# Deeper loading of raw 64-bit weights in the first block, borrowed homes for three of seven, and a last block ordered by segments

## The chip, the cores and the metric

The kernel runs on one core of a Trainium2 chip. The metric is the device time of one execution in microseconds, and what stands for a kernel is the median over its runs. Before the change that is 948.53 us, the median of 3 runs that lie between 947.35 and 951.66 us.

## The reference, cut to what matters

```
q, k, v: (4, 8, 576, 64) float32
q_d, k_d, v_d = mean over groups of 4 positions              # 144 positions
out_up    = repeat(softmax(q_d k_d^T / 8) v_d, 4)            # coarse attention
out_local = softmax over |i - j| < 4 of (q k^T / 8), times v # banded attention
x = (out_up + out_local) as (2304 tokens, 512)
g = x @ w_gate;  x2 = (silu(g) * (x @ w_val)) @ w_out        # 512 -> 1536 -> 512
h = x2 @ w_in
out = (h * clip(h + 3, 0, 6) / 6) @ w2_out                   # 512 -> 2048 -> 512
```

The five weight matrices arrive as 64-bit floats; everything else is 32-bit.

## The kernel before, in words

**Blocks.** The 2304 tokens are 36 units of 64 tokens. `BLOCKS = [8, 6, 8, 8, 6]` cuts them into five blocks of 512 or 384 tokens. The tokens of batch 0 (9 units) are computed by `first_batch`, whose instructions stand in the order of the table `FRONT`; the attention of the other batches runs beside the matrix products of the block before the one that needs it. It is cut into chunks (`CUTS`): for each, `load_chunk` issues loads of q, k and v on SyncE's queue, `chunk_scores` multiplies q by seven shifted k on VectorE (tile `pr`, line 852) and reduces (`sc`, line 855).

**Products.** Each block runs 68 weight units of 12 matmuls (9 for P in a 384-token block): G and V (gate and value, `pG`, `pV`), O (first output, `aO`), H (second input, `pH`), P (second output, `aP`). They are numbered through, so 4 and 5 are G, 6 and 7 V, 8 and 9 O, 10 and 11 G, 12 and 13 V, 14 and 15 O. Every weight is split into a high and a low part of type fp32r, every input too, and three of the four partial products are made.

**The way of a weight in block 0.** `load_raw` loads the 64-bit words (512 KB a unit, tile `w64`, four buffers; line 220) on SyncE's queue, `decode_a` takes the sign and exponent on ScalarE (`top`, line 237), `decode_b` makes 32-bit words on VectorE (`w`, line 246; it also frees the raw buffer), `split_hi` (ScalarE, `wr`, line 264) and `split_lo` (VectorE, `wr`, line 269) make the two parts for a pair of units, and ScalarE's queue writes the 32-bit pair to DRAM (`kept`). Blocks 1 to 4 load the kept pair (512 KB) and split it again. `prefetch(i)` does these steps for units ahead of i: loading by `LR = 8`, decoding by 5 and 4, splitting by 3.

**What else matters here.** `first_batch` keeps the softmax weights in `held`, a tile in the buffer of `x2`, and a temporary `tmp` in one of the two buffers of `xr`, the columns of the block's input. `x2` holds the output of the first network at the end of a block's first half, and `os`, the output, takes its buffer after that. Instructions stay in program order on their engine; a DMA that waits for its buffer holds up all behind it on SyncE's queue. `put_out` copies 128 output rows from PSUM (line 1073 on VectorE for odd quarters of the last block, 1075 on ScalarE) and stores them (line 1084).

Of the kernel before, what the change touches and what calls it, by code (L numbers as in the profile page):

```python
# [11 lines left out]
F32 = mybir.dt.float32  # L12
F32R = mybir.dt.float32r
# [14 lines left out]
BLOCKS = [8, 6, 8, 8, 6]  # L28

CUTS = [[3, 2], [2, 2, 2, 2], [3, 2, 3], [3, 3], []]  # L30
LR, LD, LA, LB, LS = 8, 6, 5, 4, 3
WARM = 14
CLOAD = (2, 6)

# [28 lines left out]
def tile_kernel(  # L63
# [124 lines left out]
    w32 = {}  # L188
    split = {}

    def load_raw(i):
        if units[i][2] == 0:
            load_unit(i)
# [5 lines left out]
    def load_unit(i):  # L199
        kind, f, bi = units[i]  # L200
        if bi or not wide:
            if i % 2 == 0:
                w32[i // 2] = sp.tile([P, 2, DM], F32, tag="wst", name=f"w32_{i}", bufs=3)
        if bi:
            if i % 2 == 0:
                nc.sync.dma_start(w32[i // 2], kept[i % NU // 2])
            return
        src = wsrc[kind]
        if wide:
            src = src.bitcast(I16)  # L210
        m = 4 if wide else 1
        if kind in "GVH":
            h = i % 2
            src = src[h * DM // 2:(h + 1) * DM // 2, (f - h) * P * m:(f - h + 2) * P * m]
            src = src.rearrange("(c p) f -> p c f", p=P)
        else:
            src = src[f * P:(f + 1) * P, :].rearrange("p (c e) -> p c e", c=2)
        if wide:
            raw[i] = sp.tile([P, 4 * DM + 32], I16, tag="w64", name=f"w64_{i}", bufs=4)
            behind(nc.sync.dma_start(raw[i][:, 1:1 + 4 * DM].rearrange("p (c e) -> p c e", c=2), src))  # L220
        else:
            nc.sync.dma_start(w32[i // 2][:, i % 2].rearrange("p (c e) -> p c e", c=2), src)
# [49 lines left out]
        split[i], split[i + 1] = r[:, 0], r[:, 1]  # L272

    def prefetch(i):
        steps = ((LR, load_raw), (LD, load_kept), (LA, decode_a), (LB, decode_b), (LS, split_unit))
        for ahead, fn in steps:
            if i + ahead < len(units):
                fn(i + ahead)
# [18 lines left out]
    xr = {}  # L297
    x_done = [0]

    def columns(bi, col, xv):  # L300

        if bi not in xr:
            xr[bi] = sp.tile([P, NC, 2, UMAX * UT], F32R, tag="xr", name=f"xr{bi}")
        return xr[bi][:, :, :, col:col + xv.shape[2]]

    def put_cols(bi, col, xv):

        dst = columns(bi, col, xv)
        nc.scalar.activation(dst[:, :, 0], xv, AF.Copy)  # L309
        nc.vector.tensor_tensor(dst[:, :, 1], xv, dst[:, :, 0].bitcast(F32), op=ALU.subtract)  # L310

# [51 lines left out]
    def first_batch():  # L363
# [6 lines left out]
        with tc.tile_pool(name="fp", bufs=1) as fp:  # L370
# [307 lines left out]
            def X(i):  # L678
                t0 = i * QT
                for cs, ps in ps_of["v", i]:  # L680
                    a = 0
                    while a < QT:
                        bi = max(m for m in range(NB) if starts[m] * UT <= t0 + a)
                        e = min(QT, starts[bi + 1] * UT - t0)
                        yield bi, cs, columns(bi, t0 + a - starts[bi] * UT, ps[:, :, a:e]), ps[:, :, a:e]
                        a = e

            def Xh(i, first=True):
# [96 lines left out]
            ))  # L785

    first_batch()
    front[0] = False


# [109 lines left out]
    def step_x(limit):  # L900

        if not xq or xq[0][0] not in down_done or xq[0][0] * NG + xq[0][1] >= limit or xq[0][4] + XLAG > tick_no[0]:
            return
        b, u, i, o, _ = xq.popleft()
        gu = b * NG + u
        px = bank("px", f"px{gu}")[:, :2 * P].rearrange("p (j c h s) -> p j c h s", j=2, c=NC, h=2)
        for j in range(2):
            t = 4 * i + 2 * j
            nc.tensor.transpose(
                px[:, j].rearrange("p c h s -> p (c h s)"), o[:, t:t + 2, :].rearrange("p t d -> p (t d)"), ident,  # L910
            )

        def evac():
            xf = ap.tile([P, NC, 2, 2, NSEG], F32, tag="xf", name=f"xf{gu}")
            for tp in range(2):
                for par in range(2):
                    rows = slice(par * D, par * D + D)
                    nc.vector.tensor_tensor(  # L918
                        xf[rows, :, :, tp, :].rearrange("p c j s -> p j c s"),
                        px[tp * D:tp * D + D, :, :, par, :],  # L920
                        odT[b][rows, u][:, None].to_broadcast([D, 2, NC, NSEG]),
                        op=ALU.add,
                    )
            bi = max(m for m in range(NB) if starts[m] <= gu)
            put_cols(bi, (gu - starts[bi]) * UT, xf.rearrange("p c j t s -> p c (j t s)"))
            x_done[0] += 1

        defer(1, evac)
# [137 lines left out]
    def put_out(bi, e, ps):  # L1066
# [2 lines left out]
            done = sp.tile([P, NC, 2, UMAX * UT], F32R, tag="x2", name=f"os{bi}", bufs=1).bitcast(F32)  # L1069
            state["os"] = done.rearrange("p c a t -> p (c a t)")  # L1070
        os = state["os"][:, e * DM:(e + 1) * DM]
        if e % 2 and bi == NB - 1:
            nc.vector.tensor_copy(os, ps)
        else:
            nc.scalar.activation(os, ps, AF.Copy)
# [2 lines left out]
        for n, m in ((0, 2),) if b == b1 else ((0, 1), (1, 1)):  # L1078
            b, u = divmod(gu + n, NG)
            if b == 0:  # L1080
                dst = out[(gu + n) * UT:(gu + n + m) * UT, :]
            else:
                dst = flat(out, (b * S + u * 4) * DM, [[DM, 4 * m], [SL * DM, NSEG], [1, DM]])
            nc.sync.dma_start(dst, os[n * UT:(n + m) * UT, :])
# [130 lines left out]
```

## Time and profile before

| | us |
|---|---|
| median of 3 runs | 948.53 |
| the profiled execution's own time | 947.45 |
| its span, first to last instruction | 945.7 |
| TensorE matmuls busy | 932.0 |
| VectorE busy | 731.7 |
| ScalarE busy | 505.3 |

The profiled execution took 947.45 us, 1.75 us more than its span and 1.08 us less than the median of the runs. TensorE is busy in 99% of the span, so what a change can win is in the short stretches in which TensorE waits, in the part ahead of the first product and in the tail behind the last. A matmul's end is modelled; the starts of the stretches tell more than their lengths.

### The profile page before, as it was taken

To read this page: it belongs to the slowest core of one execution; us is meant where nothing else is said; L and a number is where in the kernel's file an instruction comes from. 1 tells how busy PE (TensorE), PEld (TensorE's weight loads), DVE (VectorE), ACT (ScalarE), POOL (GpSimd) and SP (SyncE) were. 2 spreads that over 40 slices of the span, in tenths; PEclk is the share of its full clock that TensorE was granted. 3 is DMA by queue.
4 is the path that set the end of the run, shared out by engine and by line. 5 is a ranking of instruction groups with operands and counts; after the bars stand their busy time and mean duration, and the time that the engine had idled before them with its cause. 6 is when DMAs were issued, how large, how long until landed. Compare 5 with 4: busy or idle time off the path is not lost.

```text
span 945.7 us, 13226 instructions
## 1 busy us (share of the span) xinstructions
PE 932.0 (99%) x4945; PEld 793.7 (84%) x4945; DVE 731.7 (77%) x1067; ACT 505.3 (53%) x945; POOL 105.8 (11%) x117
## 2 busy tenths in 40 slices
PE   8999999999999999999999999999999999999997
PEld 6887887788899988978888778888888888999996
DVE  6969989798889979998835899995447994545652
ACT  5964677877534586453335764533335445434542
POOL 6420022000153100027300000000000000000000
PEclk9999999999999999999999999999999999999999
DMA  9898899678899732579932223542232224434331
GB/s 223 174 305 314 301 347 308 192 267 295 290 239 215 163 108 69 191 219 181 200 112 89 68 90 130 196 141 91 92 109 89 89 90 131 143 128 134 131 114 34
DMA packets 100048, 160.80 MB, mean 170 GB/s; under 512 B 53368, under 2 KB 57080, under 8 KB 99984
## 3 DMA queue, kind: packets, MB, share of 16 engines
q1 hardware_dynamic: 57680, 131.43, 43.6%
q0 software_dynamic: 37408, 10.71, 10.6%
q10 hardware_dynamic: 4896, 17.83, 4.7%
q8 instruction: 39, 0.64, 0.3%
q14 instruction: 25, 0.20, 0.1%
HBM read 137.31 MB, written 22.54 MB: 169 GB/s over the span
## 4 chain that ended last, share of the span: by engine, by line
PE 72%; DVE 11%; DMA 8%; ACT 4%; issue 3%; POOL 1%; SPq 1%; ACTq 0%; POOLq 0%; DVEq 0%
PE aO L1050 15%; PE pV L358 15%; PE aP L1050 14%; PE pG L358 14%; PE pH L358 12%; DMA twok<-in_k_dram 3%; DVE wr L269 2%; DMA k<-in_k_dram 2%; DMA w<-in_moe_w_out_dram 1%; DVE pv L889 1%; DVE xf L918 1%; DVE h L1024 1%; DVE gH L1026 1%; SPq L147 1%; DVE pv L893 1%
## 5 line engine op out<-in xcount | busy, mean ns | idle before, releaser
L269 DVE TENSOR_TENSOR wr<-w,wr 128x1024 fp32r<-128x1024 f32 x170 | 207.6, 1221 | 118.0 <-ACT wr L264 117.6
L264 ACT ACTIVATE wr<-w 128x1024 fp32r<-128x1024 f32 x170 | 179.4, 1056 | 117.7 <-issue 54.1
L1050 PE MATMUL aP<-wr,gH 128*128 128x512 f32 x864 | 211.4, 395 | 1.4 <-ACT gH L1025 0.8
L358 PE MATMUL pH<-x,wr 128*128 128x512 f32 (+1 forms) x960 | 211.3, 371 | 0.7 <-DVE wr L269 0.4
L358 PEld LDWEIGHTS pH<-x,wr 128*128 128x128 f32 x960 | 173.3, 188 | 26.0 <-issue 2.1
L1050 PEld LDWEIGHTS aP<-wr,gH 128*128 128x128 f32 x864 | 159.6, 188 | 36.2 <-ACT gH L1025 1.6
L358 PE MATMUL pG<-xr,wr 128*128 128x512 f32 (+1 forms) x720 | 153.6, 368 | 0.8 <-ACT xr L309 0.8
L358 PE MATMUL pV<-xr,wr 128*128 128x512 f32 (+1 forms) x720 | 153.4, 368 | 0.9 <-ACT sl L1014 0.9
L1050 PE MATMUL aO<-gV,wr 128*128 128x512 f32 (+1 forms) x720 | 152.7, 368 | 0.0
L358 PEld LDWEIGHTS pV<-xr,wr 128*128 128x128 f32 x720 | 130.9, 188 | 18.2 <-ACT sl L1014 1.4
L358 PEld LDWEIGHTS pG<-xr,wr 128*128 128x128 f32 x720 | 130.8, 188 | 18.3 <-ACT xr L309 1.2
L1050 PEld LDWEIGHTS aO<-gV,wr 128*128 128x128 f32 x720 | 130.8, 188 | 16.7
L1023 ACT ACTIVATE h<-pH,consts 128x512 f32<-128x512 f32 (+1 forms) x80 | 51.3, 642 | 52.7 <-PE pH L358 52.5
L1025 ACT ACTIVATE gV<-sl 128x512 fp32r<-128x512 f32 (+1 forms) x60 | 35.0, 584 | 67.5 <-DVE sl L1020 67.4
L1014 ACT ACTIVATE sl<-pG 128x512 f32<-128x512 f32 (+1 forms) x60 | 33.2, 554 | 70.5 <-PE pG L358 70.4
L1025 ACT ACTIVATE gH<-h 128x512 fp32r<-128x512 f32 (+1 forms) x80 | 46.8, 586 | 44.6 <-DVE h L1024 44.4
L237 ACT ACTIVATE top<-w 128x512 f16<-128x512 bf16 x68 | 53.3, 794 | 16.6 <-DVE w L246 4.7
L852 DVE TENSOR_TENSOR pr<-q,k 128x1792 f32<-128x1792 f32 x27 | 54.5, 2019 | 9.8 <-DMA k<-in_k_dram 9.7
L1024 DVE SCALAR_TENSOR_TENSOR h<-h,pH 128x512 f32<-128x512 f32 (+1 forms) x80 | 50.5, 631 | 13.3 <-ACT h L1023 12.6
L1026 DVE TENSOR_TENSOR gH<-h,gH 128x512 fp32r<-128x512 f32 (+1 forms) x80 | 50.5, 632 | 11.6 <-ACT gH L1025 11.5
L889 DVE TENSOR_TENSOR pv<-sc,v 128x1792 f32<-128x1792 f32 x27 | 54.6, 2021 | 0.5
L855 DVE TENSOR_REDUCE sc<-pr 128x28 f32<-128x1792 f32 x27 | 54.4, 2013 | 0.2
(137 smaller groups left out, 754.1 us busy)
## 6 DMA issues: line engine op xcount, KB each, us to landing
w<-kept SPq DMA_DIRECT2D x136, 512.0 KB
kept<-w ACTq DMA_DIRECT2D x34, 512.0 KB
w<-in_moe_w_out_dram SPq DMA_DIRECT2D x28, 512.0 KB
w<-in_moe_w_in_dram SPq DMA_DIRECT2D x16, 512.0 KB
w<-in_moe_w_gate_dram SPq DMA_DIRECT2D x12, 512.0 KB
w<-in_moe_w_val_dram SPq DMA_DIRECT2D x12, 512.0 KB
out_dram<-os SPq DMA_DIRECT2D x16, 256.0 KB
dnv<-in_v_dram POOLq DMA_DIRECT2D x24, 144.0 KB, 7.1
```

The costliest lines, as they stand in the source:

```text
L237: behind(nc.scalar.activation(halves(top[i % 2], 2, F16)[:, :, 1], h3.bitcast(BF16), AF.Copy))
L264: behind(nc.scalar.activation(parts[i][:, 0], w32[i // 2].rearrange("p u e -> p (u e)"), AF.Copy))
L269: behind(nc.vector.tensor_tensor(r[:, 1], s, r[:, 0].bitcast(F32), op=ALU.subtract))
L358: nc.tensor.matmul(ps, r[:, a, c], x[:, c, b_, :ps.shape[1]], start=part is HIGH and a == c == 0, stop=part is LOW and c == NC - 1,)
L852: nc.vector.tensor_tensor(pr, qt[:, a:a + SUB, None, :].to_broadcast([P, SUB, W, D]), win(kt, a, SUB), op=ALU.mult)
L855: nc.vector.tensor_reduce(sc[:, a:a + SUB], pr, axis=AX.X, op=ALU.add)
L889: nc.vector.tensor_tensor(pr, pe[:, a:a + SUB, :, None].to_broadcast([P, SUB, W, D]), win(vt, a, SUB), op=ALU.mult)
L1023: nc.scalar.activation(h, ps, AF.Relu, scale=1 / 6, bias=half1[:, 0:1])
L1024: nc.vector.scalar_tensor_tensor(h, h, 1.0, ps, op0=ALU.min, op1=ALU.mult)
L1025: nc.scalar.activation(g[:, 0, :nt], h, AF.Copy)
L1026: nc.vector.tensor_tensor(g[:, 1, :nt], h, g[:, 0, :nt].bitcast(F32), op=ALU.subtract)
L1050: nc.tensor.matmul(ps, **one, start=f_ == 0 and a == b_ == 0, stop=f_ == nf - 1 and b_ == 1,)
```

## The change

It has three parts.

1. Raw loads run 11 units ahead, not 8. Units 0 to 7 use the four `w64` buffers as before; from unit 8 on every seven units take three homes inside a borrowed tile and four `w64` buffers. The borrowed tile is `raws0` (printed `rawsFalse`) in the buffer of `x2` for units 8 to 38 and `raws1` (`rawsTrue`) in a buffer of `xr` from unit 43 on. In `prefetch` the raw load now stands behind `decode_b`. Units 8, 9 and 10 are loaded at the end of `first_batch`.
2. The columns of the last block are ordered by segment: the 128 columns of a pair of units run over (segment, unit, position), so the 8 rows that belong together in the output lie side by side. The evacuations write with strides, and the output store has the outer dimensions 16 x 8 where it had 8 x 16.
3. The last 128 output rows are copied half by VectorE and half by ScalarE.

```diff
-LR, LD, LA, LB, LS = 8, 6, 5, 4, 3
+LR, LD, LA, LB, LS = 11, 6, 5, 4, 3
+RAW0, RAWS, MORE = 8, 4, 3
...
+    def raw_home(i):
+        n = (i - RAW0) % (RAWS + MORE)
+        if i < RAW0 or n >= MORE:
+            return sp.tile([P, 4 * DM + 32], I16, tag="w64", name=f"w64_{i}", bufs=RAWS)
+        half = i >= NU1 + MORE
+        if half not in homes:
+            homes[half] = sp.tile(
+                [P, NC, 2, UMAX * UT], F32R, tag=("x2", "xr")[half], name=f"raws{half}", bufs=(1, 2)[half],
+            ).bitcast(I16).rearrange("p c a t -> p (c a t)")
+        m = 4 * DM + 32
+        return homes[half][:, n * m:(n + 1) * m]
...
-            raw[i] = sp.tile([P, 4 * DM + 32], I16, tag="w64", name=f"w64_{i}", bufs=4)
+            raw[i] = raw_home(i)
...
-        steps = ((LR, load_raw), (LD, load_kept), (LA, decode_a), (LB, decode_b), (LS, split_unit))
+        steps = ((LD, load_kept), (LA, decode_a), (LB, decode_b), (LR, load_raw), (LS, split_unit))
...
-        dst = columns(bi, col, xv)
+        dst = columns(bi, col, UT)
+        if bi == NB - 1:
+            e, r = divmod(col // UT, 2)
+            dst = columns(bi, e * P, P).rearrange("p c a (s u t) -> p c a s u t", s=NSEG, u=2)[:, :, :, :, r]
...
     first_batch()
+    for i in range(RAW0, LR):
+        load_raw(i)
...
-        if e % 2 and bi == NB - 1:
+        if bi == NB - 1 and e == BLOCKS[bi] * UT // P - 1:
+            h = DM // 2
+            nc.vector.tensor_copy(os[:, :h], ps[:, :h])
+            nc.scalar.activation(os[:, h:], ps[:, h:], AF.Copy)
+        elif e % 2 and bi == NB - 1:
...
+            elif bi == NB - 1:
+                dst = flat(out, (b * S + u * 4) * DM, [[SL * DM, NSEG], [DM, 4 * m], [1, DM]])
             else:
                 dst = flat(out, (b * S + u * 4) * DM, [[DM, 4 * m], [SL * DM, NSEG], [1, DM]])
```

The first place is SyncE's queue where block 0 begins. `q1_0` and `k1_0` are the q and k of the first attention chunk of batch 1; `w64_8` is the raw load of unit 8, and so on. Before:

```order
L220 DMA w64_8_1007<-in_moe_w_out_dram 128x2048
L220 DMA w64_9_1029<-in_moe_w_out_dram 128x2048
L220 DMA w64_10_1037<-in_moe_w_gate_dram 128x2x1024
L147 DMA q1_0_1042<-in_q_dram 128x768
L147 DMA k1_0_1044<-in_k_dram 128x1152
L220 DMA w64_11_1063<-in_moe_w_gate_dram 128x2x1024
L220 DMA w64_12_1088<-in_moe_w_val_dram 128x2x1024
L220 DMA w64_13_1108<-in_moe_w_val_dram 128x2x1024
```

The same place of the changed kernel, where the first two rows are units 8, 9 and 10 in their borrowed homes:

```order
L235 DMA rawsFalse_989<-in_moe_w_out_dram 128x2048 x2
L235 DMA rawsFalse_989<-in_moe_w_gate_dram 128x2x1024
L235 DMA w64_11_1014<-in_moe_w_gate_dram 128x2x1024
L235 DMA w64_12_1035<-in_moe_w_val_dram 128x2x1024
L235 DMA w64_13_1044<-in_moe_w_val_dram 128x2x1024
L148 DMA q1_0_1046<-in_q_dram 128x768
L148 DMA k1_0_1048<-in_k_dram 128x1152
L235 DMA w64_14_1069<-in_moe_w_out_dram 128x2048
```

The raw loads of units 11, 12 and 13 now stand ahead of the chunk's q and k on the queue.

The second place is VectorE at the same time, in the changed kernel: `pr1_0_0` is the first product of that chunk, `wr8` the low part of units 8 and 9, `w32_10` the decoding of 10 and 11.

```order
L261 SCALAR_TENSOR_TENSOR w32_8_1093<-rawsFalse_989,top1_161 128x512
L872 TENSOR_TENSOR pr1_0_0_1133<-q1_0_1046,k1_0_1048 128x1792
L284 TENSOR_TENSOR wr8_1114<-w32_8_1093,wr8_1114 128x1024
L875 TENSOR_REDUCE sc1_0_1132<-pr1_0_0_1133 128x28
L261 SCALAR_TENSOR_TENSOR w32_10_1138<-rawsFalse_989,top0_159 128x512
L1042 TENSOR_TENSOR sl0_2_1109<-sl0_2_1109,pV0_2_1145 128x512
```

And VectorE at that place before:

```order
L246 SCALAR_TENSOR_TENSOR w32_8_1091<-w64_9_1029,top1_161 128x512
L852 TENSOR_TENSOR pr1_0_0_1131<-q1_0_1042,k1_0_1044 128x1792
L269 TENSOR_TENSOR wr8_1112<-w32_8_1091,wr8_1112 128x1024
L855 TENSOR_REDUCE sc1_0_1130<-pr1_0_0_1131 128x28
L246 SCALAR_TENSOR_TENSOR w32_10_1138<-w64_10_1037,top0_159 128x512
L1020 TENSOR_TENSOR sl0_2_1106<-sl0_2_1106,pV0_2_1144 128x512
```

Nothing moved here but the raw tile's name: the chunk's product still stands ahead of the low part of units 8 and 9.

## Rows read from the trace of the kernel before

**Rows 1.** The page, its part 1: busy time, share of the span, instructions.
```profile
PE 932.0 (99%) x4945; PEld 793.7 (84%) x4945; DVE 731.7 (77%) x1067; ACT 505.3 (53%) x945; POOL 105.8 (11%) x117
```

**Rows 2.** TensorE's timeline in block 0: start, us, group, idle before.
```profile
69.71 5.60 PE L358 MATMUL pV<-xr,wr 128*128 128x512 f32 x24
75.15 5.61 PE L1050 MATMUL aO<-gV,wr 128*128 128x512 f32 x24
...
80.81 5.71 PE L358 MATMUL pG<-xr,wr 128*128 128x512 f32 x24
...
87.66 6.07 PE L358 MATMUL pV<-xr,wr 128*128 128x512 f32 x24 [0.88 <-ACT sl L1014]
```

**Rows 3.** TensorE's timeline at the end of block 0.
```profile
241.92 6.58 PE L1050 MATMUL aP<-wr,gH 128*128 128x512 f32 x27
249.03 5.34 PE L1050 MATMUL aP<-wr,gH 128*128 128x512 f32 x21 [0.53 <-ACT gH L1025]
254.20 2.09 PE L358 MATMUL pG<-xr,wr 128*128 128x384 f32 x11
```

**Rows 4.** The chain that ended last, 28 to 95 us: start, length, what.
```profile
42.91 18.88 DMA twok<-in_k_dram
...
64.02 6.62 DMA k<-in_k_dram
```

**Rows 5.** VectorE's timeline, 67 to 91 us.
```profile
70.75 2.02 DVE L852 TENSOR_TENSOR pr<-q,k 128x1792 f32<-128x1792 f32 x1 [2.46 <-DMA k<-in_k_dram]
72.70 1.22 DVE L269 TENSOR_TENSOR wr<-w,wr 128x1024 fp32r<-128x1024 f32 x1
...
86.20 1.22 DVE L269 TENSOR_TENSOR wr<-w,wr 128x1024 fp32r<-128x1024 f32 x1
```

**Rows 6.** ScalarE's timeline, 72 to 87 us.
```profile
72.74 0.79 ACT L237 ACTIVATE top<-w 128x512 f16<-128x512 bf16 x1 [2.23 <-DMA w<-in_moe_w_gate_dram]
...
86.39 0.78 ACT L237 ACTIVATE top<-w 128x512 f16<-128x512 bf16 x1 [1.55 <-DMA w<-in_moe_w_out_dram]
```

**Rows 7.** SyncE's queue, issues by time from 36 us on.
```profile
55.36 3.33 SPq L220 DMA_DIRECT2D w<-in_moe_w_out_dram  x2
61.34 0.38 SPq L220 DMA_DIRECT2D w<-in_moe_w_gate_dram  x1
...
65.39 3.30 SPq L220 DMA_DIRECT2D w<-in_moe_w_val_dram  x2
```

**Rows 8.** Windows: PE, PEld, DVE, ACT, POOL busy; clock; DMA share; GB/s.
```profile
60.00:62.00 2.00, 2.00 (x10) 1.65 (x9) 1.66 (x2) 1.88 (x3) 0.91 (x2) 1.00 0.93 330
...
64.00:66.00 2.00, 2.00 (x10) 1.65 (x10) 2.00 (x5) 1.31 (x3) 0.00 (x0) 1.00 0.84 235
66.00:68.00 2.00, 2.00 (x11) 1.65 (x10) 2.00 (x3) 2.00 (x4) 0.00 (x0) 1.00 1.01 290
68.00:70.00 2.00, 2.00 (x11) 1.65 (x10) 0.30 (x1) 1.49 (x3) 0.00 (x0) 1.00 1.00 406
```

**Rows 9.** VectorE's timeline at the end of block 0.
```profile
240.82 2.02 DVE L852 TENSOR_TENSOR pr<-q,k 128x1792 f32<-128x1792 f32 x1 [2.30 <-DMA k<-in_k_dram]
```

**Rows 10.** The tail on all engines, from 939 us.
```profile
939.29 0.60 ACT L1075 ACTIVATE os<-aP 128x512 f32<-128x512 f32 x1 [2.12 <-PE aP L1050]
```

**Rows 11.** ScalarE by line and shape: busy, mean ns, idle before.
```profile
L1014 ACT ACTIVATE sl<-pG 128x512 f32<-128x512 f32 x36 | 21.4, 596 | 46.0 <-PE pG L358 45.9
L1014 ACT ACTIVATE sl<-pG 128x384 f32<-128x384 f32 x24 | 11.8, 492 | 24.5 <-PE pG L358 24.4
```

**Rows 12.** SyncE's queue, two stores: block 0's last and the kernel's last.
```profile
255.03 0.33 SPq L1084 DMA_DIRECT2D out_dram<-os  x1
...
939.91 0.60 SPq L1084 DMA_DIRECT2D out_dram<-os  x1
```

**Rows 13.** Windows of one us in the tail, columns as in rows 8.
```profile
942.00:943.00 1.00, 0.00 (x0) 0.00 (x0) 0.00 (x0) 0.00 (x0) 0.00 (x0) 1.00 0.56 152
943.00:944.00 1.00, 0.00 (x0) 0.00 (x0) 0.00 (x0) 0.00 (x0) 0.00 (x0) 0.58 0.44 168
```

More of the change, by code (lines that the diff above doesn't have):

```diff
@@ L189, in tile_kernel @@
     split = {}
+    homes = {}
+    def raw_home(i):
[9 more added lines that the diff above has]
+        return homes[half][:, n * m:(n + 1) * m]
     def load_raw(i):
@@ L298, in tile_kernel, with columns @@
     x_done = [0]
-    def columns(bi, col, xv):
+    def columns(bi, col, n):
         if bi not in xr:
             xr[bi] = sp.tile([P, NC, 2, UMAX * UT], F32R, tag="xr", name=f"xr{bi}")
-        return xr[bi][:, :, :, col:col + xv.shape[2]]
+        return xr[bi][:, :, :, col:col + n]
     def put_cols(bi, col, xv):
-        dst = columns(bi, col, xv)
+        dst = columns(bi, col, UT)
+        if bi == NB - 1:
+            e, r = divmod(col // UT, 2)
+            dst = columns(bi, e * P, P).rearrange("p c a (s u t) -> p c a s u t", s=NSEG, u=2)[:, :, :, :, r]
         nc.scalar.activation(dst[:, :, 0], xv, AF.Copy)
@@ L684, in X @@
                         e = min(QT, starts[bi + 1] * UT - t0)
-                        yield bi, cs, columns(bi, t0 + a - starts[bi] * UT, ps[:, :, a:e]), ps[:, :, a:e]
+                        yield bi, cs, columns(bi, t0 + a - starts[bi] * UT, e - a), ps[:, :, a:e]
                         a = e
@@ L913, in evac @@
         def evac():
-            xf = ap.tile([P, NC, 2, 2, NSEG], F32, tag="xf", name=f"xf{gu}")
+            bi = max(m for m in range(NB) if starts[m] <= gu)
+            xf = ap.tile([P, NC, UT], F32, tag="xf", name=f"xf{gu}")
+            by = "p c (s j t) -> p c j t s" if bi == NB - 1 else "p c (j t s) -> p c j t s"
+            xs = xf.rearrange(by, j=2, t=2, s=NSEG)
             for tp in range(2):
@@ L918, in evac @@
                     nc.vector.tensor_tensor(
-                        xf[rows, :, :, tp, :].rearrange("p c j s -> p j c s"),
+                        xs[rows, :, :, tp, :].rearrange("p c j s -> p j c s"),
                         px[tp * D:tp * D + D, :, :, par, :],
@@ L923, in evac @@
                     )
-            bi = max(m for m in range(NB) if starts[m] <= gu)
-            put_cols(bi, (gu - starts[bi]) * UT, xf.rearrange("p c j t s -> p c (j t s)"))
+            put_cols(bi, (gu - starts[bi]) * UT, xf.rearrange("p c (s t) -> p c s t", t=4) if bi == NB - 1 else xf)
             x_done[0] += 1
```

## The prediction, made before the changed kernel had run

> **What bounds the kernel now.** I read the page first. TensorE is busy in 99% of the span [rows 1], so time can be won or lost only where its products start late. Next I read TensorE's timeline block by block, by starts: a stretch of 24 matmuls of 512 columns takes 75.15 - 69.71 = 5.44 us when nothing holds it up [rows 2]. In block 0 two places are late because of data. The products of units 12 and 13 start at 87.66 after 0.88 us of idle, put down to ScalarE [rows 2]. ScalarE had stood at a `top` that waited for the raw load of unit 15 until 86.39 [rows 6], but VectorE's low part of units 12 and 13 also ended only at 86.20 + 1.22 = 87.42 [rows 5]. The second place is the end of the block: 48 matmuls from 241.92 to 254.20 take 12.28 us where two stretches take 10.88, so 1.4 us are lost [rows 3]. VectorE had waited there 2.30 us for the k of the next chunk [rows 9], and the loads of the last raw units stand ahead of that k on the queue. The rest of block 0's losses are switches between kinds of matmuls that the change does not touch. So the deeper loading can win some 2 us at most, and I looked for what it puts in the way.
>
> **Part 1, the raw loads.** The data that SyncE's queue moves is the same, and no engine gets an instruction more. What moves is the order on the queue. Before, the first chunk's k was issued at 64.02 and landed 6.62 us later, at 70.64 [rows 4], behind the loads of units 8, 9 and 10, the last of which was issued at 61.34 [rows 7]. VectorE waited 2.46 us for it and began the chunk's product at 70.75 [rows 5]. In the changed queue, units 8, 9 and 10 need no buffer that decoding gives back, only the end of `first_batch`'s reads of `held`; and units 11, 12 and 13 take the buffers that decoding of 4, 5 and 6 gives back, which is what let units 8, 9 and 10 go at 55.36 (two) and 61.34 (one) before [rows 7]. So three more loads of 512 KB are on the queue by 61.7, and q and k stand behind them. They can't be issued sooner than before, because their tiles lie over `first_batch`'s, whose last Pool load ends at 42.91 + 18.88 = 61.79 [rows 4].
>
> How much later does k land? A lower bound is zero, if the three loads found idle transfer time earlier. The windows speak against most of that: the transfer engines are busy 0.93 of 60 to 62 us, 0.84 of 64 to 66 and 1.0 of 66 to 70 [rows 8], so from 60 on the idle time is 0.14 + 0.32 = some 0.5 us. An upper bound is three times what one raw load took behind k: unit 11's landed by 72.74 [rows 6], some 2.0 us after k's product began at 70.75 [rows 5], so 3 x 2.0 = 6.0 us. Between them: the mean of the two full windows is (290 + 406) / 2 = 348 GB/s [rows 8], and 3 x 524 KB = 1.57 MB take 4.5 us at that; minus the 0.5 us of idle time that they fill, 4.0; plus some 0.3 for the write of one more kept pair that now shares the time. I take **4.3 us**, nearer to the upper bound because the windows are full.
>
> What is queued behind it: VectorE takes its instructions in order, and behind the chunk's product stands the low part of units 8 and 9, then everything up to the low part of units 12 and 13 [rows 5]. From 70.75 to 87.42 VectorE has 16.7 us of work and no wait that the change could take away, so if it begins 4.3 us later, the low part of 12 and 13 ends at 91.7. TensorE feels it twice. Units 8 and 9 started at 75.15 [rows 2], with their low part done at 72.70 + 1.22 = 73.92 [rows 5]: the 1.2 us between are slack, so they start 4.3 - 1.2 = 3.1 us late. Units 12 and 13 start right behind 91.7, at about 91.9 where it was 87.66: **4.2 us** late. The old wait of 0.88 us is inside that number, for ScalarE no longer waits for raw data there. Nothing gives these 4.2 us back, since TensorE has no idle time in which to catch up.
>
> At the end of block 0 the last raw loads are done three units, or 3 x 2.72 = 8.2 us, earlier, and the next chunk's k has fewer of them ahead. It was 2.30 us late [rows 9]; I take most of the 1.4 us back: **-1.0 us** (between 0 and -1.4).
>
> The borrowed buffers cost nothing that I can find. The output of the first network needs `x2`'s buffer only when all of units 8 to 38 are decoded, and VectorE must have decoded 38 for a product at that same time anyway; if that cover went, ScalarE's copies of the first network's output would stand and all of H behind them. `raws1` waits for the last V product of block 0 and holds up the queue behind it, chunk v among them, but its first unit is decoded six units or some 16 us later; without that cover the price would be one transfer, about 2 us.
>
> **Parts 2 and 3, the tail.** The last copy on ScalarE starts at 939.29 and takes 0.60 [rows 10]. ScalarE's copies from PSUM take 596 ns at 512 columns and 492 at 384 [rows 11], so 104 ns for 128 columns and some 0.39 us at 256: -0.2 us. The store behind it takes 0.60 us to issue, where block 0's contiguous store takes 0.33 [rows 12]: -0.25 if the new shape issues like that one, 0 if not. In the tail the transfer engines are busy 0.56 and 0.44 of the windows at 152 and 168 GB/s [rows 13], which is half of 16, as the outer dimension of 8 would have it. At 160 GB/s the 262 KB of a store take 1.64 us, and on twice the engines 0.82: -0.8 us, between 0 and -1.6. The sum of the tail is **-1.25 us**. The strided writes of the last block's columns are the same instructions on as many elements, made during block 3, where TensorE never waits for them; uncovered, one pair of them would cost under a microsecond.
>
> Here a rule can be set beside the row. The Trainium skill, "DMA: Bandwidth & Descriptors", section "Anatomy of one DMA", gives a transfer a fixed part of about 2.0 us that nothing shortens, plus bytes at 436 GB/s. By it the data part of 262 KB on all engines is an estimated 0.6 us and 1.2 us on half of them, so this term would be -0.6, not -0.8, and the sum 0.2 us higher; the row's own rate is used.
>
> **The sum.** 4.2 - 1.0 - 1.25 = +1.95 us. The profiled execution took 947.45 us, 1.75 more than its span, so one like it comes to 949.4. The median of the runs is 1.08 us above the profiled one, at 948.53, and gives 950.5. I predict **950.0 us**. About 0.5%, or 4.7 us, is what a measurement of this kernel can tell from no change.
>
> **The rivals.**
>
> *The chunk's k is hidden after all.* The three loads fill gaps that a mean over 16 engines does not show, and k lands less than 1 us late. Then the wait of 0.88 us goes, and the sum is -0.9 - 1.0 - 1.25 = -3.1: 945.4 us. For it speak that unit 8, 9 and 10 may go some 7 us sooner than before; against it the shares of 0.93 to 1.0.
>
> *Slower: the wait puts TensorE's clock down.* If k is 6 us late or more, TensorE stands about 5 us ahead of units 8 and 9. In the tail its granted clock reads 0.58 of full speed, so the lower level of 1.2 GHz for most of that microsecond, in the window from 943 to 944, after idling since 939.3 [rows 13]. The next 24 matmuls would take up to 10.9 us, not 5.44, and as part of that lies in VectorE's time I price it at 3 to 5 us: 6.0 - 1.0 - 1.25 + 4 = +7.7, so 956 us. [...] The Trainium skill, "TensorE: Matmul & The Clock Gate", Part 1, says the same of an idle engine: its clock goes to half until it has been busy again.
>
> *The loads do not run ahead.* SyncE's queue could stand at a buffer, a landing or `held`, so that units 11 to 13 go no sooner than q and k could have. Their places on the queue are fixed, so k would then be issued later still, by up to 3 us against 64.02, and land as late as in the forecast: 949 to 952 us. What would fail is only the gain at the end of the block.
>
> **How the numbers follow.** Forecast 0.56 (947.5 to 952.5 us by its own bounds), k hidden 0.26, clock 0.12, no running ahead 0.06. The range reaches down to the hidden case and up to where the clock case begins: 945.0 to 954.0, which leaves out about a tenth at each end. Faster by over 0.5% needs below 943.8, so more than every late start that I found: 0.06, the low end of the hidden case. Slower needs above 953.3: the clock case and the forecast's upper end, 0.14. The rest, 0.80, is within 0.5%.
>
> **What would show it.** VectorE's first `pr` starts at 74 to 76 us, not 70.75, with a wait of 6 to 8 us put down to k; the O product of units 8 and 9 starts near 78, and the V product of 12 and 13 near 92, without ScalarE's raw wait. At the end of block 0, 48 matmuls of P take about 11.3 us. In the tail the transfer share is near 1.0 and the store issues in 0.33 us. I am wrong if `pr` starts before 72, if the O product starts on time although `pr` is late, if the clock falls near 80 us, or if a wait for `x2` or `xr` shows where there was none.

## The result, and the profile after

The changed kernel takes 953.58 us, the median of 7 runs between 952.45 and 957.59; the kernel before, 948.53 over as many. The ratio is 1.0052, with a 95% interval of 1.0031 to 1.0072: slower by half a per cent. The profiled execution took 952.62 us with a span of 950.9, 5.2 us more than the span before. The time lies inside the range I gave (945 to 954), but at its upper end: past the 953.3 us that I called slower, and outside the forecast's own bounds (947.5 to 952.5). The sum was 1.95 us where the span shows 5.2. So I looked for what the sum had missed.

TensorE's timeline of the changed kernel in block 0 (start, us, group, idle before) answers to [rows 2]:

```profile
53.24 5.74 PE L376 MATMUL pG<-xr,wr 128*128 128x512 f32 x24
...
75.29 0.39 PE L1072 MATMUL aO<-gV,wr 128*128 128x512 f32 x1
77.71 7.16 PE L1072 MATMUL aO<-gV,wr 128*128 128x512 f32 x23 [2.04 <-DVE wr L284]
...
84.92 5.73 PE L376 MATMUL pG<-xr,wr 128*128 128x512 f32 x24
...
90.71 6.00 PE L376 MATMUL pV<-xr,wr 128*128 128x512 f32 x24
```

Units 10 and 11 start at 84.92, not 80.81: 4.11 us late. Of that, 2.04 us are the wait for the low part of units 8 and 9. The 23 matmuls behind it take 7.16 us where 24 take 5.6, and the windows (columns as in [rows 8]) say why: the granted clock falls to 0.50. Units 12 and 13 start at 90.71, not 87.66: 3.05 us late, for the wait that stood ahead of them before the change is gone and gives 1.06 us back.

```profile
76.00:78.00 2.00, 0.29 (x1) 0.29 (x2) 2.00 (x3) 0.00 (x0) 0.00 (x0) 1.00 1.03 419
78.00:80.00 2.00, 2.00 (x8) 1.60 (x8) 2.00 (x2) 0.00 (x0) 0.00 (x0) 0.80 0.64 247
80.00:82.00 2.00, 2.00 (x6) 1.54 (x5) 2.00 (x5) 1.73 (x3) 0.00 (x0) 0.50 0.18 36
```

VectorE's timeline, to set beside [rows 5]: the chunk's first product and the low part behind it.

```profile
74.50 2.03 DVE L872 TENSOR_TENSOR pr<-q,k 128x1792 f32<-128x1792 f32 x1 [4.21 <-DMA k<-in_k_dram]
76.44 1.22 DVE L284 TENSOR_TENSOR wr<-w,wr 128x1024 fp32r<-128x1024 f32 x1
```

So the product starts 3.75 us late (74.50 against 70.75), where I had forecast 4.3. But SyncE's queue, to set beside [rows 7], shows another reason than mine:

```profile
48.91 0.84 SPq L235 DMA_DIRECT2D rawsFalse<-in_moe_w_out_dram  x2
50.77 0.38 SPq L235 DMA_DIRECT2D rawsFalse<-in_moe_w_gate_dram  x1
55.33 0.38 SPq L235 DMA_DIRECT2D w<-in_moe_w_gate_dram  x1
58.32 3.09 SPq L235 DMA_DIRECT2D w<-in_moe_w_val_dram  x2
69.17 0.34 SPq L148 DMA_DIRECT2D q<-in_q_dram  x1
69.56 0.54 SPq L148 DMA_DIRECT2D k<-in_k_dram  x1
```

k is issued 5.5 us later than before (69.56, not 64.02 [rows 4]) and then lands sooner after its issue: its product starts 4.9 us later, where the transfer took 6.62. What released the issue is Pool (GpSimd). The waits of SyncE's queue from 60 to 75 us (us in total, times, longest) name it; line 148 issues q and k:

```profile
SPq L148 <- DMA twok<-in_k_dram: 5.1, 1, 5.1
SPq L148 <- POOL dnk L741: 2.3, 1, 2.3
```

Pool's timeline in the changed kernel, the two additions of block pairs of k that `first_batch` ends with:

```profile
61.18 1.30 POOL L741 TENSOR_TENSOR dnk<-twok 72x512 f32<-72x512 f32 x1 [7.53 <-DMA twok<-in_k_dram]
66.79 2.35 POOL L741 TENSOR_TENSOR dnk<-twok 72x512 f32<-72x512 f32 x1 [4.31 <-DMA twok<-in_k_dram]
```

and in the kernel before:

```profile
59.46 1.30 POOL L723 TENSOR_TENSOR dnk<-twok 72x512 f32<-72x512 f32 x1 [5.80 <-DMA twok<-in_k_dram]
61.85 1.75 POOL L723 TENSOR_TENSOR dnk<-twok 72x512 f32<-72x512 f32 x1 [1.09 <-DMA twok<-in_k_dram]
```

The last addition waits for Pool's own load `twok` and starts 4.9 us later. It ends at 66.79 + 2.35 = 69.14, and q, with k behind it, goes at 69.17.

At the end of block 0, TensorE's timeline of the changed kernel, to set beside [rows 3], and on into block 1:

```profile
245.21 0.48 PE L1072 MATMUL aP<-wr,gH 128*128 128x512 f32 x1
246.95 11.47 PE L1072 MATMUL aP<-wr,gH 128*128 128x512 f32 x47 [1.26 <-DVE wr L284]
258.25 4.35 PE L376 MATMUL pG<-xr,wr 128*128 128x384 f32 x24
262.44 4.33 PE L376 MATMUL pV<-xr,wr 128*128 128x384 f32 x24
267.81 2.37 PE L376 MATMUL pG<-xr,wr 128*128 128x384 f32 x12 [1.04 <-DVE sl L1042]
```

48 matmuls take 258.25 - 245.21 = 13.04 us, not 12.28, and block 1 has a new wait for VectorE. VectorE's timeline there, to set beside [rows 9]:

```profile
243.13 0.69 DVE L261 SCALAR_TENSOR_TENSOR w<-rawsTrue,top 128x512 int32<-128x512 int32 x1 [4.51 <-DMA kept<-w]
243.74 2.02 DVE L872 TENSOR_TENSOR pr<-q,k 128x1792 f32<-128x1792 f32 x1
```

The wait for k is gone, and one of 4.51 us for the write of a kept pair stands ahead of the product, whose buffer the decoding needs. Such a wait was there before the change too, but shorter:

```profile
236.69 0.69 DVE L246 SCALAR_TENSOR_TENSOR w<-w,top 128x512 int32<-128x512 int32 x1 [1.36 <-DMA kept<-w]
```

VectorE stood 1.36 + 2.30 = 3.66 us there before, and 4.51 now. The chain of waits of the changed kernel gives the write its length:

```profile
234.39 8.62 DMA kept<-w
```

In the tail, the last copies of the changed kernel, to set beside [rows 10]:

```profile
946.19 0.42 DVE L1096 COPY os<-aP 128x256 f32<-128x256 f32 x1 [0.67 <-PE aP L1072]
946.64 0.39 ACT L1097 ACTIVATE os<-aP 128x256 f32<-128x256 f32 x1 [2.58 <-DVE os L1096]
```

ScalarE's half starts when VectorE's is done. From the first copy's start to the end of the span it is 950.9 - 946.2 = 4.7 us, where it was 945.7 - 939.3 = 6.4 [rows 10].

Block 2 starts at 418.82 in the changed kernel:

```profile
418.82 5.51 PE L376 MATMUL pG<-xr,wr 128*128 128x512 f32 x23 [0.80 <-ACT xr L327]
```

and at 412.07 before:

```profile
412.07 5.72 PE L358 MATMUL pG<-xr,wr 128*128 128x512 f32 x24 [0.78 <-ACT xr L309]
```

So the account of the 5.2 us, from these starts: 3.05 by units 12 and 13; 0.76 in block 0's last stretch; 0.24 between the two (258.25 - 254.20 = 4.05 in all); 6.75 - 4.05 = 2.70 in block 1; 0.15 in blocks 2 to 4 (the last copy starts 6.90 later); and -1.7 in the tail.

### The profile page after: what moved, and what is told of

Read it like the earlier page. It is cut to its first block, busy times and chain, and to the rows that moved or that the text cites. A ratio compares the mean times of both kernels' runs of the same rounds, so it can differ in the third digit from the quotient of the medians.

```text
span 950.9 us, 13208 instructions
## 1 busy us (share of the span) xinstructions
PE 934.6 (98%) x4945; PEld 794.6 (84%) x4945; DVE 735.0 (77%) x1068; ACT 504.0 (53%) x945; POOL 106.3 (11%) x117
## 4 chain that ended last, share of the span: by engine, by line
PE 79%; DVE 9%; ACT 4%; DMA 3%; issue 2%; SPq 1%; ACTq 0%; DVEq 0%
PE aP L1072 17%; PE pH L376 16%; PE aO L1072 14%; PE pG L376 13%; PE pV L376 13%; DVE wr L284 2%; DMA kept<-w 2%; PE fO L160 1%; DVE pr L872 1%; DVE sc L875 1%; DVE w L261 1%; ACT wr L279 1%; DMA w<-kept 1%; ACT pd L779 1%; PE pO L801 1%
## 5 line engine op out<-in xcount | busy, mean ns | idle before, releaser
L1072 PE MATMUL aO<-gV,wr 128*128 128x512 f32 (+1 forms) x720 | 154.8, 371 | 2.0 <-DVE wr L284 2.0
L1048 DVE TENSOR_TENSOR gV<-sl,gV 128x512 fp32r<-128x512 f32 (+1 forms) x60 | 39.0, 650 | 9.6 <-ACT gV L1047 9.5
```

The lines of the kernel that those rows point to most:

```text
L1048: nc.vector.tensor_tensor(g[:, 1, :nt], h, g[:, 0, :nt].bitcast(F32), op=ALU.subtract)
L1072: nc.tensor.matmul(ps, **one, start=f_ == 0 and a == b_ == 0, stop=f_ == nf - 1 and b_ == 1,)
```

## The experiments

Two theories of the front: **A**, mine of before, that k lands late because three raw loads stand ahead of it on SyncE's queue; **B**, that raw loads running early slow Pool's `twok`, which lets k be issued. For the end of block 0: that the chunk's loads slow the kept write. The kernel before, run beside them on the same chips, had medians from 947.7 to 948.6 us.

**late8: the early loads in units 0 to 2.**

```diff
-    for i in range(RAW0, LR):
-        load_raw(i)
+RAMP = {0: [8, 9], 1: [10, 11], 2: [12, 13]}   # load_raw of these in prefetch
```

> Undoes the early loading of raw units 8 to 10: units 8 to 13 are issued two at a time in units 0, 1 and 2 of block 0, still ahead of the first chunk's q and k. Theory A (the loads in the queue ahead of k delay it, as predicted): the queue order is as in the changed kernel, so k lands at 74 to 75 us, pr starts at 74.5 and the time stays within 1 us of the changed kernel. Theory B (the raw loads at 49 to 51 us slow the Pool queue's accumulating loads, which free k's tile late): the last twok lands back near 62, k is issued near 64, pr starts at 71 to 73, and 1.5 to 3 us of the 5 lost come back.

954.06 us (ratio to the kernel before 1.0050, interval 1.0027 to 1.0074). It did not do what it was for: the borrowed homes wait for `held` alone, so units 8 to 10 went at 49.16 to 50.55 all the same. Pool's last addition came still later, at 70.75, k was issued at 72.45, and the product started at 76.74.

**early8: q and k ahead of units 12 and 13 on the queue.**

```diff
+RAMP = {0: [11], 1: [], 2: [], 3: [12, 13], 4: [14], 5: [15, 16], 6: [17]}
```

> Keeps units 8 to 10 early (49 to 51 us) and 11 behind them, but puts the first chunk's q and k ahead of raw units 12 and 13. Theory A: two of three loads are gone from ahead of k, so pr starts 2.5 us earlier than in the changed kernel, near 72. Theory B: the Pool loads are as late as in the changed kernel, 65 to 67 us, k is issued near 69 and pr starts at 73.5 to 75; no time is won, and raw units 12 and 13 come later.

958.98 us (1.0106, 1.0073 to 1.0139). k was issued at 68.77 and the product started at 73.52, as B has it; A had it near 72. VectorE's order had also changed, which the edit was not meant to do: the product stood ahead of work that TensorE needs sooner, and the wait for k reached TensorE after half of a G.

```profile
77.41 5.36 PE L380 MATMUL pG<-xr,wr 128*128 128x512 f32 x12 [10.46 <-DVE sl L1046]
```

**both: one unit at a time, then q and k, then the rest.**

```diff
-    for i in range(RAW0, LR):
-        load_raw(i)
+RAMP = {0: [8], 1: [9], 2: [10], 3: [11, 12], 4: [13, 14], 5: [15, 16], 6: [17]}
```

> Units 8, 9 and 10 are loaded as before the change (one each in units 0 to 2) and q and k stand ahead of 11 to 13; from unit 3 on the loads catch up to 11 ahead, two a unit. Both theories: pr starts at 70.5 to 71.5 us and the 3 us lost at units 12 and 13 come back, 950 to 951 us. What it then tells is how much of the remaining loss lies at the end of block 0 (the decoding that waited 4.5 us for a kept pair) and in block 1: if those come from the front, all is gone and the time is 947 to 948; if they come from the deeper loading itself, 1.5 to 2.5 us stay.

959.78 us (1.0131, 1.0096 to 1.0166), not the 950 to 951 that I expected. Again units 8 to 10 went early (48.77 to 52.05) and VectorE's order changed: the product started at 70.84, as before the change, but stood ahead of work that TensorE then waited 9.91 us for. With units 11 to 13 behind q and k, k was still issued only at 66.52. As times the two runs tell nothing about the theories, since the order moved too; what they leave is that k's issue follows Pool's addition and not the loads ahead of it on the queue.

**seg_only: the last block by segments alone**, no deeper loading, the last copy whole.

```diff
-LR, LD, LA, LB, LS = 11, 6, 5, 4, 3
+LR, LD, LA, LB, LS = 8, 6, 5, 4, 3
```

> The kernel before with the last block's columns by segment and the 16 x 8 store alone; raw loads as before, the last copy whole on ScalarE. From the tails of both profiles: the last landing comes 1.9 us sooner after its issue and the copy does not lose 0.25 us, so 946.0 to 947.0 us, about 2 us below the kernel before. If the tail's gain belonged to the halved copy, nothing would change.

946.53 us (0.9983, 0.9962 to 1.0004). The last copy starts at 941.92 and the span ends at 946.4: a tail of 4.5 us against 6.4, a gain of 1.9. The time's own interval reaches 1, so the gain is read from the tail.

**gate_behind and gate_ahead: truly late loads.** A memset of two columns of each home, in order behind the decoding, makes units 8 to 10 wait as before the change. In the first, units 11 to 13 still stand ahead of q and k; in the second they stand behind, and have a gate too.

```diff
             raw[i] = raw_home(i)
+            if RAW0 <= i < RAW0 + MORE:    # + 7 in gate_ahead
+                tc.keep_in_program_order(nc.vector.memset(raw[i][:, 1:3], 0))
...
+RAMP = {0: [8, 11], 1: [9, 12], 2: [10, 13]}                                    # gate_behind
+RAMP = {0: [8], 1: [9], 2: [10], 3: [11], 4: [12, 13], 5: [14, 15], 6: [16, 17]}  # gate_ahead
```

> The changed kernel with the raw loads of units 8, 9 and 10 made to wait for the decoding of units 4, 5 and 6, as before the change, by a tiny VectorE memset of each home; units 11 to 13 still stand ahead of the first chunk's q and k. Theory A (order on SyncE's queue): nothing changes against the changed kernel, since the same six loads stand ahead of k; k lands at 74 to 75 and VectorE's first chunk product starts at 74 to 75. Theory B (the early loads slow the Pool queue's accumulating loads, whose end lets q and k go): those loads end at about 62 as before, k is issued at 63.5 to 66 and the product starts at 71 to 74, somewhere between: if it starts below 72.5 the queue order was not a cause at all. In both the end of block 0 is as in the changed kernel. Time by A 953.5, by B 950 to 952.

> As the kernel with gates, but on the queue q and k of the first chunk stand ahead of units 11 to 13 as before the change, and the loads get to 11 units ahead only after it. Both theories: k is issued at 64, the chunk's first product starts at 70.5 to 72, and the first block loses nothing at its front (units 12 and 13 start near 88). What is left of the 5.2 us of span then belongs to the end of block 0 and to block 1: if the wait for the kept pair there comes from the chunk's loads standing close to it and not from what the front did, the 48 matmuls of the last output stretch take 13.0 us again, and the time is about 950; if the late front caused it, they take 12.3 or less, and the time is 947 to 948.

948.27 us (0.9999, 0.9978 to 1.0020) and 947.92 us (1.0000, 0.9977 to 1.0022). Pool's timeline of gate_behind:

```profile
59.07 1.30 POOL L747 TENSOR_TENSOR dnk<-twok 72x512 f32<-72x512 f32 x1 [7.69 <-DMA twok<-in_k_dram]
65.69 1.95 POOL L747 TENSOR_TENSOR dnk<-twok 72x512 f32<-72x512 f32 x1 [5.32 <-DMA twok<-in_k_dram]
```

and of gate_ahead:

```profile
59.06 1.30 POOL L747 TENSOR_TENSOR dnk<-twok 72x512 f32<-72x512 f32 x1 [3.21 <-DMA twok<-in_k_dram]
60.69 1.37 POOL L747 TENSOR_TENSOR dnk<-twok 72x512 f32<-72x512 f32 x1 [0.33 <-DMA twok<-in_k_dram]
```

Up to there the two differ in the loads of units 11 to 13; Pool issued its loads of `twok` at the same time in both (41.8), and its last addition starts 5.0 us apart. B's expectation for gate_behind (62) failed, since it blamed units 8 to 10 alone: units 11 to 13 do it here, as 8 to 10 did in the run `both`. k was issued at 68.06 and 62.47. In gate_ahead the product started at 68.71 with no wait, and units 12 and 13 ran 33.6 us after the first G product, against 34.4 before: the front loses nothing. Its expectation also asked whether the late front had caused the wait at the end of block 0. It had not: VectorE stood 4.36 us at the kept write again, the 48 matmuls took 12.91 us and block 1 161.0. The time came back to 947.92, not to 950, because block 0 up to that stretch is 2.0 us shorter than before the change (186.6 against 188.7 us from the first G) and the tail shorter as well.

In gate_behind the product was as late as in the changed kernel (21.3 us after the first G in both), and the time, 948.27, was below what either theory gave. VectorE's timeline there:

```profile
70.02 1.23 DVE L287 TENSOR_TENSOR wr<-w,wr 128x1024 fp32r<-128x1024 f32 x1 [0.21 <-ACT wr L282]
73.95 2.03 DVE L876 TENSOR_TENSOR pr<-q,k 128x1792 f32<-128x1792 f32 x1 [2.71 <-DMA k<-in_k_dram]
```

The low part of units 8 and 9 now stands ahead of the product, which I had not asked for. TensorE's waits at G and V were 0.8 us each, and units 12 and 13 came 35.0 us after the first G, where the changed kernel has 37.5. So the price of a late k seems to hang on what VectorE's order puts behind it. That was tried by itself.

**low_first: this swap alone, in the changed kernel.**

```diff
+        if i == 8:
+            tc.keep_in_program_order(low)    # the low part of 8 and 9
...
+            if (b, c, a) == (1, 0, 0):
+                tc.keep_in_program_order(ins)    # the chunk's first product
```

> The changed kernel with one swap on VectorE: the low part of units 8 and 9 (and one decoding of unit 10) stand ahead of the chunk's first product, as they came to stand in the kernel with gates whose loads stood ahead of q and k. The loads, and so k, are as late as in the changed kernel: the product starts at 74 to 76 us, with a wait on k. If the late k costs TensorE its time through the low part queued behind the product, the O product of units 8 and 9 now starts on time, some 21.9 us after the first G product (24.5 in the changed kernel, 21.9 before), units 12 and 13 are 1 to 2 us late and not 3 to 4, and the time is 950.5 to 952.5. If the low part of units 8 and 9 is not what O waits for, O stays late and the time stays at 953 to 954.

951.46 us (1.0024, 1.0003 to 1.0045), as expected, though its interval overlaps the changed kernel's. TensorE's timeline shows half of the expectation right:

```profile
74.64 5.61 PE L1077 MATMUL aO<-gV,wr 128*128 128x512 f32 x24
...
83.71 0.49 PE L379 MATMUL pG<-xr,wr 128*128 128x512 f32 x1 [3.21 <-ACT wr L279]
84.97 7.13 PE L379 MATMUL pG<-xr,wr 128*128 128x512 f32 x23 [0.77 <-DVE wr L284]
```

O is on time; the wait moved to the next G, since k was later still in this execution (product at 76.82). Units 12 and 13 came 39.4 us after the first G, so no nearer than in the changed kernel. This execution took 953.94 us, the longest of its twelve, so what the swap is worth stays open.

**early4 and early4_b0: the chunk's loads two units later**, at the end of every block, and of block 0 alone.

```diff
-EARLY = 6
+EARLY = 4                                         # early4
-            if m == NU - EARLY:
+            if m == NU - (EARLY if bi else 4):    # early4_b0
```

> The changed kernel with the attention chunks' loads issued two units later (4 units ahead of their use, not 6). If these loads, on the same transfer engines, are what made the write of the last kept pair of block 0 take 8.6 us and VectorE's decoding wait 4.5 us for it, that wait falls below 2 us and the 48 matmuls at the end of block 0 take 11.5 to 12.3 us, not 13.0: 1 us saved in block 0, unless the chunk's own k becomes late, which would show as a new wait of VectorE on k. If the write is slow for another reason (its queue, the raw loads), the 13.0 us stay. The front is as in the changed kernel, perhaps 0 to 2 us later. Time 952 to 955.

> The changed kernel with the chunk's loads two units later at the end of block 0 alone (the run that did it in every block won there and lost 4.1 us in block 2). The front is as in the changed kernel: q and k issued at 69 to 70, 3 to 4 us lost. By the theory of the kept write the end of block 0 and block 1 give back 1.6 + 2.7 = 4.3 us: 949 to 950. If it is not so, 953 to 954.

953.61 us (1.0048, 1.0029 to 1.0066) and 949.50 us (1.0014, 1.0002 to 1.0026). Both lost the kept write's wait; SyncE's queue and TensorE's timeline in early4_b0:

```profile
236.35 8.94 SPq L221 DMA_DIRECT2D w<-kept  x2
245.34 0.42 SPq L148 DMA_DIRECT2D q<-in_q_dram  x1
```

```profile
248.84 11.18 PE L1072 MATMUL aP<-wr,gH 128*128 128x512 f32 x48
259.86 2.44 PE L376 MATMUL pG<-xr,wr 128*128 128x384 f32 x13
```

The last stretch takes 259.86 - 248.84 = 11.02 us, and block 1 158.1, not 160.6. early4 gained as much there (11.01 us, and 157.8 in block 1) and lost it in block 2, which took 203.1 us where the changed kernel's took 198.9. The first G of early4's profiled execution was 5.7 us late for a reason of its own (TensorE stood 2.33 us at a load of v, and its granted clock fell), so its front is not compared.

**nosplit: the last copy whole.**

```diff
-        if bi == NB - 1 and e == BLOCKS[bi] * UT // P - 1:
-            h = DM // 2
-            nc.vector.tensor_copy(os[:, :h], ps[:, :h])
-            nc.scalar.activation(os[:, h:], ps[:, h:], AF.Copy)
-        elif e % 2 and bi == NB - 1:
+        if e % 2 and bi == NB - 1:
```

> The changed kernel with the last 128 rows copied whole by VectorE, not in halves. The two halves ran one after the other, ScalarE waiting for VectorE, and ended 0.88 us after the last matmul where one copy ended 0.64 us after it: so 0.2 to 0.3 us less between the last matmul and the store's issue, and a time 0.2 us lower, which is below what the medians tell. If the halves had gained something, the tail gets longer by 0.2 us.

953.76 us (1.0049, 1.0033 to 1.0065). The tail from the copy's start is 950.7 - 946.21 = 4.5 us, with ScalarE as the copier, not VectorE as I had written.

```profile
946.21 0.60 ACT L1097 ACTIVATE os<-aP 128x512 f32<-128x512 f32 x1 [2.12 <-PE aP L1072]
```

The halves end at 946.64 + 0.39 = 947.03, 0.84 us after the first one's start: they cost 0.24 us.

**best and shallow.** gate_ahead with early4_b0 and nosplit; and seg_only with early4_b0, so without depth.

> The kernel with q and k ahead of units 11 to 13 and gates, and in addition the chunk's loads at the end of block 0 alone two units later, and the last copy whole. Theory: the chunk's loads share the transfer engines with the last kept pair's write, VectorE's decoding waits 4.4 us for that write, and what VectorE is late by comes out once in block 0's last stretch (1.4 us) and again in block 1 (3.1 us more than before the change). Then the wait is gone, 48 matmuls take 11.0 to 11.3 us, block 1 takes 157.8 to 158.5 and not 161.0, the span is 941 to 942.5 and the time 942.5 to 945. Rival: the wait only moves to the chunk's k, as in the forecast's kernel before; then block 1 keeps its 161 us and the time stays at 947 to 948.

> No deeper raw loading at all (8 units, four buffers), the last block by segments, and the chunk's loads at the end of block 0 two units later. If the deeper loading brings something of its own, this stays above the kernel that has it, at 945 to 947, with the wait of VectorE for the chunk's k (2.3 us before) still there or longer, since the last raw loads stand ahead of k. If the depth brings nothing, both come out within a microsecond of each other.

best: 944.49 us (0.9970, 0.9957 to 0.9983), faster than both kernels. Block 0's last stretch was clean, as expected; block 1 was not, at 160.6 us, and the span of 945.4 missed the 941 to 942.5 that I expected. (This execution took 947.06 us, the longest of its eleven.) TensorE's timeline:

```profile
241.91 11.15 PE L1076 MATMUL aP<-wr,gH 128*128 128x512 f32 x48
252.90 4.35 PE L382 MATMUL pG<-xr,wr 128*128 128x384 f32 x24
...
264.84 0.62 PE L1076 MATMUL aO<-gV,wr 128*128 128x384 f32 x2 [1.35 <-ACT wr L282]
```

ScalarE's timeline shows what this wait hangs on, the load of a kept pair:

```profile
263.73 1.06 ACT L282 ACTIVATE wr<-w 128x1024 fp32r<-128x1024 f32 x1 [2.64 <-DMA w<-kept]
```

ScalarE of early4_b0 had such waits too (1.06 and 2.82 us), and block 1 took 158.1 us there; why they cost more in best stays open. The first G of this execution was also 1.7 us later than in the kernel before.

shallow: 945.88 us (0.9981, 0.9961 to 1.0000). Its interval overlaps that of best, so that deeper loading brings anything of its own is not shown as a time. In the profiles, block 0 from its first G to block 1 takes 198.0 us in best, 199.6 in shallow and 200.9 in the kernel before, one execution each; the wait for the kept write is 3.10 us in shallow, with no deeper loading.

## Why the prediction was right or wrong

**Term A (+4.2).** The place and the sign were right, and the size came near: the product 3.75 us late (4.3 forecast), the O product of units 8 and 9 at 77.71 ("near 78"), units 12 and 13 3.05 us late (4.2). The cause was wrong, so that the size came near is luck. The failed step is "They can't be issued sooner than before, because their tiles lie over `first_batch`'s, whose last Pool load ends at ... 61.79": I took that end as fixed. It moved, and k's issue with it:

| kernel | raw loads moved forward | Pool's last add starts | k issued | product starts |
|---|---|---|---|---|
| gate_ahead | none | 60.69 | 62.47 | 68.71 |
| shallow | none | 60.80 | 62.94 | 70.06 |
| seg_only | none | 60.96 | 63.56 | 71.54 |
| before | none | 61.85 | 64.02 | 70.75 |
| both | 8 to 10 | 64.85 | 66.52 | 70.84 |
| gate_behind | 11 to 13 | 65.69 | 68.06 | 73.95 |
| changed | 8 to 13 | 66.79 | 69.56 | 74.50 |
| early8 | 8 to 11 | 67.1 | 68.77 | 73.52 |
| low_first | 8 to 13 | 69.23 | 70.95 | 76.82 |
| nosplit | 8 to 13 | 69.97 | 71.69 | 75.96 |
| late8 | 8 to 13 | 70.75 | 72.45 | 76.74 |
| early4_b0 | 8 to 13 | 72.19 | 73.89 | 78.10 |

In each of them q goes 0.02 to 0.04 us after that addition's end, with k right behind it. The table also shows how far one execution speaks: with the same six loads forward the addition starts anywhere from 66.8 to 72.2, so the direction is shown, and the 5.0 us between the gates is one pair of executions. Two kernels are not in the table: in best, with none forward and a first G 1.7 us later than before, it starts at 63.30; in early4, where units 10 and 11 were themselves loaded late (54.11 and 60.60), at 64.09. The three raw loads ahead of k did not lengthen its own way: 4.9 us from issue to product in the changed kernel and 5.9 in gate_behind, against 6.62 to its landing before. I had read the windows from 60 us on. Those ahead of it, of the kernel before,

```profile
50.00:54.00 4.00, 4.00 (x39) 3.43 (x39) 2.21 (x5) 1.62 (x5) 1.65 (x1) 1.00 1.17 303
54.00:58.00 4.00, 4.00 (x19) 3.27 (x18) 1.41 (x3) 2.78 (x4) 0.00 (x0) 1.00 1.18 295
```

show a transfer share over 1, as the profile counts it, there already: what I moved forward pushed back Pool's queue. The Trainium skill, "DMA: Bandwidth & Descriptors", section "Queues, rings and completion order", says that each transfer engine takes turns between the queues that have work for it; the two Pool timelines of the gates agree, with 5.0 us between them for three loads of 512 KB on another queue.

**How TensorE felt it.** I forecast a wait of 3.1 us at units 8 and 9 and put no clock loss into the sum; I left the clock to a rival in which k is 6 us late or more and TensorE stands about 5 us. The product was 3.75 us late, the wait was 2.04 us, and the clock fell: 7.16 us for 23 matmuls, some 1.7 more than at full clock. So the rival's mechanism came with the forecast's, and the second step that failed is that condition; I had it from one row of the tail. The lower clock shows only when TensorE is at work again, 1.00 in 76 to 78 us and 0.50 in 80 to 82. "Nothing gives these 4.2 us back" failed as well: units 8 and 9 cost 4.11, and 1.06 came back at units 12 and 13, which no longer had a wait of their own. The Trainium skill, "TensorE: Matmul & The Clock Gate", Part 1, has an idle engine's clock go to half until it has been busy again, and the trace agrees with that, at 0.50. The runs behind it agree on the rest of the step: what stands on VectorE behind the product waits (early8, both), and what stands ahead does not (gate_behind, low_first). What that order is worth as a time is not shown.

**Term B (-1.0).** Measured +0.76. VectorE no longer waited for k, but it also came to k 2.9 us later than before (243.74, not 240.82), so that k landed sooner is not shown. The failed step is "I take most of the 1.4 us back", which let the wait for k go and put nothing in its place. Six loads of chunks now leave in one burst from 233.2 to 236.1 us, the kept write took 8.62 us beside them, and VectorE stood 4.51 us at a buffer that it frees, where it had been 1.36. With the chunk's loads two units later, that wait is gone (early4_b0, 1.0014 of the kernel before where the changed kernel has 1.0052: some 3.6 us).

**Block 1 (+2.70)** was in no term. It is at least in part the same wait, carried on: VectorE's lateness came out once in block 0's last stretch and again behind it. The two kernels that only move the chunk's loads have 157.8 and 158.1 us there, against 157.9 before. But best has 160.6 without that wait, so something else can cost the same, and how the 2.70 us divide stays open.

**Term C (-1.25).** Measured -1.7. The transfer is the term that was under-sized: seg_only's tail, with a store that still takes 0.54 us to issue, gained 1.9 us where I had 0.8 in a range to 1.6. A window in the tail of the changed kernel, to set beside [rows 13]:

```profile
947.00:948.00 1.00, 0.00 (x0) 0.00 (x0) 0.00 (x0) 0.03 (x1) 0.00 (x0) 1.00 0.74 213
```

The share is 0.7, not near 1 as I had written, but more than the half of before. The Trainium skill, "DMA: Bandwidth & Descriptors", section "Why a DMA increments its semaphore by 16 and not by 1", has the outermost dimensions of a transfer decide over how many engines it runs; the rows agree, with half of 16 busy at 8 outer rows and 0.7 at 16. The estimate of -0.6 was the further from -1.9; the page gives its fixed part and rate for transfers that GpSimd issues, and this store goes out on SyncE's queue. The issue gained next to nothing:

```profile
947.05 0.54 SPq L1112 DMA_DIRECT2D out_dram<-os  x1
```

0.54 us, not 0.33. And the halved copy, -0.2 in my sum, cost 0.24: its halves did not run side by side.

**Borrowed buffers.** Nearly as forecast: no engine waits for `x2`'s or `xr`'s buffer. SyncE's queue does stand 0.9 us at the last V product of block 0, near 146 us, before it may load into `raws1`; VectorE, ScalarE and TensorE have no wait for a load from there to 175 us, so it cost nothing that shows. But "cost nothing" was wrong in another way: because the homes were free, units 8 to 10 could go at 49 us, where the transfer share was 1.17.

## What to carry to other kernels

Before a load is moved forward, read the transfer share where it will now run, and ask which other queue has loads under way whose landing frees a buffer; here that queue, and not the one that was changed, set the delay. A wait in front of an in-order engine costs what is queued behind it, so ask for its place in that engine's order as well as for its length. Read more than one execution before giving such a delay a size. When a wait is removed, look at what else is due in the same few microseconds; here it was a write whose buffer was needed next.

## What the runs showed of the hardware

Three raw loads of 512 KB more on SyncE's queue went with a later end of Pool's loads: its last addition started at 65.69 us, not 60.69 (gate_behind and gate_ahead). With six more it started between 66.8 and 72.2.

TensorE's granted clock fell to 0.50 of full speed, the lower of its two levels, behind a recorded idle time of 2.04 us in the changed kernel; behind 1.99 us in block 1 of gate_behind it also read 0.50 (264 to 266 us), behind 3.21 us in low_first 0.63 over 84 to 88. Two waits of 0.8 us at the front of gate_behind, one of 1.26 at the end of block 0 in the changed kernel and one of 1.35 in best left it at 1.00.

Two engines that copied different halves of one PSUM tile into one SBUF tile ran one after the other, with a wait of the second for the first in the trace; whether the chip or the program's semaphores ask for that was not tried.
